# Loading the v weights of an attention and GLU kernel in quarters on two queues, and moving one small norm computation

## The chip, the cores and the metric

One core of a Trainium2 chip. The metric is device time in microseconds of one execution. Most executions agree to within a few tenths of a per cent, and this study is about a few tenths of a per cent, so the scatter itself becomes a subject below. All times inside a profile are microseconds from the start of the profiled span; the span is about 1.8 us shorter than the device time of the same execution.

## The reference, cut to what matters

```
x = A_x                                   # 2048 tokens x 512
xn = layernorm(x)
A: qkv = xn @ wqkv; softmax features of q and k per head (32 heads of 16); linear attention; @ wo
B: ((xn @ w_gate) * (xn @ w_up)) @ w_down # 512 -> 1792 -> 512
return x + A(xn) + B(xn)
```

Everything works on tiles of 128 tokens (16 tiles, numbered 0 to 15). Before a tile can be multiplied it is loaded, centred and transposed.

Of the kernel before, what the change touches and what calls it, by code (L numbers as in the profile page):

```python
# [13 lines left out]
PE, ACT, DVE, POOL, SP = "PE", "ACT", "DVE", "POOL", "SP"  # L14
# [6 lines left out]
NQ = D // 128  # L21
# [104 lines left out]
def _build(nc, es, A_x, A_wqkv, A_w_phi, A_wo, B_w_gate, B_w_up, B_w_down, out):  # L126
# [142 lines left out]
    def load_x(t0, n, eng=SP):  # L269
        o = sb("x", t0 * 512, n * 512).rearrange("p (t d) -> p t d", t=n)  # L270
        i = rows(x_flat, t0, n)
        sc.dma(eng, lambda e: e.dma_start(o, i), [], [("x", t) for t in range(t0, t0 + n)], n * 131072)
# [11 lines left out]
    wv_v = sb("wv", 0, NQ * 512).rearrange("p (q j) -> p q j", q=NQ)  # L284
    wo_v = sb("wo", 0, NQ * 512).rearrange("p (q j) -> p q j", q=NQ)
# [5 lines left out]
    def load_w(eng, o, i, key, nbytes):  # L291
        sc.dma(eng, lambda e: e.dma_start(o, i), [], [key], nbytes)
# [10 lines left out]
            load_w(eng, v[:, :, sl], src[:, sl].rearrange("(q p) f -> p q f", p=128), (("wg", "wu")[k], s),  # L303
                   1024 * n)

    def load_v(eng, h):
        i = A_wqkv[h * 256:(h + 1) * 256, 1024:1536].rearrange("(q p) j -> p q j", p=128)
        load_w(eng, wv_v[:, 2 * h:2 * h + 2, :], i, ("wv", h), 262144)


    def c_fn(e):
# [11 lines left out]
    sc.pin = True  # L323
    load_x(0, 1)
    load_x(1, 1, ACT)
    load_x(2, 2)
    load_v(SP, 1)
    load_gu(SP, 0, (1,))
    act(sbf("lnv", 0, 1), eps_f, ["eps"], ["pace"])
    load_v(ACT, 0)  # L330
    load_gu(ACT, 0, (0,))
    load_gu(SP, 1)
    load_w(SP, wphi_v, bass.AP(tensor=A_w_phi.tensor, offset=A_w_phi.offset, ap=[[16, 128], [2048, NQ], [1, 16]]),
# [32 lines left out]
    def misc_bank(w=2):  # L366
        misc[0] += 1
        return 2 + misc[0] % w
# [4 lines left out]
    def w_fold(w, dt, b=None):  # L373
        b = misc_bank() if b is None else b

        def fn(e):
            ins = None
            for jt in range(NQ):
                ins = e.matmul(bank(b, jt * 128, 128), lhsT=wT_v[:, w, jt, dt * 128:(dt + 1) * 128],  # L379
                               rhs=wbd_v[:, jt, :], start=True, stop=True)  # L380
            return ins
        sc.step(PE, fn, [("wT", w, jt) for jt in range(NQ)] + [("wbd", jt) for jt in range(NQ)], [("ps", b)], 4 * 60.0)
        act(Wp_v[:, w, dt, :], bank(b), [("ps", b)], [("Wp", w, dt)])
# [91 lines left out]
    def x_transpose(t, b, h=0, parts=1, eng=ACT):  # L475
        n = NQ // parts
        qs = slice(h * n, (h + 1) * n)

        def fn(e):
            ins = None  # L480
            for i in range(n):
                q = h * n + i
                ins = e.transpose(bank16(b, i * 128, 128), xn_tile(t)[:, q * 128:(q + 1) * 128], ident)  # L483
            return ins
        sc.step(PE, fn, [("xn", t, h), "ident"], [("ps", b)], n * 60.0)
        o = sb("xnT", 0, NQ * S_TOK).rearrange("p (q s) -> p q s", q=NQ)[:, qs, t * 128:(t + 1) * 128]
        i = bank16(b, 0, n * 128).rearrange("p (q s) -> p q s", q=n)
        w = [("xnT", t, h)] if parts == 2 else [("xnT", t)]
        if eng == ACT:
            act(o, i, [("ps", b)], w)  # L490
        else:
            dve(lambda e: e.tensor_copy(out=o, in_=i), [("ps", b)], w, n * 128)
# [45 lines left out]
    def v_matmul(t, b, hs=(0, 1)):  # L538
        for h in hs:
            mm(bank(b), [(xnT(q, t * 128, 128), wv_v[:, q, :]) for q in (2 * h, 2 * h + 1)],  # L540
               ([("xnT", t, h)] if t < 2 else [("xnT", t)]) + [("wv", h)], b, start=h == 0, stop=h == 1)

    def v_keep(t, b):
        raw = sbf("vraw", (t - 2) * 512, 512)
# [103 lines left out]
    def squares(src, i, after):  # L648
        j = squared[0] % 4
        squared[0] += 1  # L650
        junk = hT_v[:, NF - 8 + 2 * j:NF - 6 + 2 * j, 3 * 512:4 * 512]
        over = [("junk", j)] if squared[0] > 4 else []
        sc.prio = 2
        if src != "wg":
            v, col, key = {"wv": (wv_v, 14 + i, [("wv", i)]), "wo": (wo_v, 16 + i, ["wo"]),
                           "wd": (wd_v, 18 + i, ["wd"])}[src]
            act(junk, v[:, 2 * i:2 * i + 2, :], key + after + over, [("junk", j), ("ssq", col)], func=ACTF.Square,
                accum=ssq[:, col:col + 1])
        else:
            i_ap = wg_v[:, :, i * 256:(i + 1) * 256].rearrange("p (a b) c -> p a b c", a=2)  # L660
            key = [(src, k) for k, (lo, n) in enumerate(SLICES) if lo < (i + 1) * 256 and lo + n > i * 256]
            act(junk.rearrange("p a (b c) -> p a b c", b=2), i_ap, key + after + over, [("junk", j), ("ssq", i)],
                func=ACTF.Square, accum=ssq[:, i:i + 1])
        sc.prio = 1
# [61 lines left out]
    def d_scale():  # L726
        norms(14, (2, 2, 7), 24)
        caps()
# [70 lines left out]
    def combine_weights(k, what=("tw", "two")):  # L799
        over = {1: [("xn", i) for i in range(4)], 2: [("Wp", 1, q) for q in range(NQ)], 3: [],  # L800
                4: [("ek", i, j) for i in range(2) for j in range(2)]}[k]
        ov_o = [("wv", 0), ("wv", 1)] if k == 1 else []
        for name, t, blk, n, src, ov in (("tw", tw, wd_block, NK, [("wdh", i) for i in range(7)], over),
                                         ("two", two, wo_block, 2, [("woh", i) for i in range(2)], ov_o)):
            if name not in what:
                continue
            i0, i1 = {1: (blk(0, 1), blk(0, 0)), 2: (blk(1, 1), t[1]), 3: (blk(1, 1), blk(0, 1)),
                      4: (blk(1, 0), t[2])}[k]
            need = {1: [], 2: [(name, 1)], 3: [(name, 1)], 4: [(name, 2)]}[k]
            dve(lambda e, o=t[k], i0=i0, i1=i1: e.tensor_tensor(out=o, in0=i0, in1=i1, op=ALU.subtract), src + need,  # L810
                [(name, k)] + ov, n * 256, 0.52)
# [218 lines left out]
    ln_center(3)  # L1030
    v_matmul(0, 0, (0,))
    v_matmul(1, 1, (0,))
    x_transpose(2, 6)
    v_matmul(0, 0, (1,))
    v_matmul(1, 1, (1,))
    for t in range(ND):
        ln_moments(t)
    (g0a, u0a, g0b, u0b), gate0 = up_unit(*ups.pop(0), pairs, 2)
# [37 lines left out]
    def scales(t):  # L1076
        last = [("hT", *latest[0])] if latest[0] else []
        for src, i in {6: [("wv", 0), ("wv", 1)], 7: [("wd", 0), ("wd", 1), ("wd", 2)],
                       8: [("wd", 3), ("wd", 4), ("wd", 5)], 9: [("wd", 6), ("wo", 0), ("wo", 1)]}.get(t, ()):
            squares(src, i, last)  # L1080
        if 2 <= t < 6:
            for i in range(2 * (t - 2), min(7, 2 * (t - 1))):
                squares("wg", i, last)
        if t in (5, 6):
            moments(range(7 * (t - 5), 7 * (t - 4)), last)
        if t == 7:
            row_of_r2(last)
            wide_row()
        if 11 <= t < 14:
            scale_weights(todo[3 * (t - 11):3 * (t - 10)], last)  # L1090
        for k, what in {14: [(1, "tw")], 15: [(3, "tw")], 16: [(2, "tw")], 17: [(1, "two"), (3, "two"), (2, "two")]}.get(t, ()):
            combine_weights(k, (what,))
        if t == 12:
            halves.extend([to_half(1), to_half(2)])
        if t >= 12:
            half_step(1)
# [26 lines left out]
    for t in range(NT + 3):  # L1123
        if t == NT + 2:
            kv_acc(t - 3)
            kv_finish()
        if t < NT:
            features("ek", t, 1)
        if t % 2 == 0 and 4 + t < NT:
            ln_stats(4 + t, 2)  # L1130
        if t > 0:
            up()
        x_next(t + 4)
        if t == 11:
            d_scale()
        late_loads(t)
        if 2 <= t - 1 < ND:
            v_place(t - 1, None)
        elif ND <= t - 1 < NT:
            b = misc_bank()  # L1140
            v_matmul(t - 1, b)
            v_place(t - 1, b)
        if t in (9, 11) or 12 <= t < NT + 1:
            if t not in (14, 16):
                up()
            if t in (9, 11, 13):
                q_next()
        if t == 7:
            w_fold(0, 2)
        scales(t)  # L1150
        if t < 2:
            v_place(t, t)
        else:
            up()
            if t == 8:
                norms(0, (7, 1), 8)
                h_scale()
                scale_row()
            if 8 <= t < NT:
                q_next()  # L1160
            if 9 <= t < 14:
                normalise(range(3 * (t - 9), min(NF, 3 * (t - 8))), [("hT", *latest[0])])
            if 3 <= t < NT + 2:
                kv_acc(t - 3)
            if t < 9:
                up()
        if 4 < t < 8:
            w_fold(0, (0, 1, 3)[t - 5])
        if t == 8:
            scaled[0] = True  # L1170
# [228 lines left out]
```

## The kernel before: the parts that the change touches

The program records steps per engine and a list scheduler in the kernel orders them when the program is built. The order on PE (TensorE) is the recorded one; DVE (VectorE), ACT (ScalarE), POOL and SP are ordered by modelled costs. In the first phase everything is "pinned" to the recorded order. The loads are issued from the queues of SP and ACT:

```
    sc.pin = True
    load_x(0, 1)              # tile 0, SP, 128 KB
    load_x(1, 1, ACT)         # tile 1, ACT
    load_x(2, 2)              # tiles 2 and 3, SP, 256 KB
    load_v(SP, 1)             # second half of the v weights, 256 KB
    load_gu(SP, 0, (1,))      # up weights, first slice
    act(sbf("lnv", 0, 1), eps_f, ["eps"], ["pace"])
    load_v(ACT, 0)            # first half of the v weights, 256 KB
    load_gu(ACT, 0, (0,))     # gate weights, first slice, 256 KB
    ...
```

The first work of PE after the transposes of tiles 0 and 1. `v_matmul(t, b, hs)` is xn of tile t times the v weights in halves of the contraction, into PSUM bank b; `g0a` and `u0a` are gate and up matmuls of block 0 for tiles 0 and 1:

```
    v_matmul(0, 0, (0,))
    v_matmul(1, 1, (0,))
    x_transpose(2, 6)
    v_matmul(0, 0, (1,))
    v_matmul(1, 1, (1,))
    ...
    g0a()
    x_transpose(3, 7)
    v_matmul(2, 2)
    v_keep(2, 2)
    u0a()
    v_matmul(3, 3)
    ...
    g1a()
    u1a()
```

In the main loop, "slot" t is one pass. Feature matmuls, v matmuls and the small norm matmuls take PSUM banks 2 and 3 in turn; each call of `misc_bank()` hands out the other one:

```
    def misc_bank(w=2):
        misc[0] += 1
        return 2 + misc[0] % w
    ...
    for t in range(NT + 3):
        ...
            features("ek", t, 1)          # takes a bank; ACT reads it with two exponentials
        ...
        x_next(t + 4)                     # normalise tile t+4 (DVE) and transpose it (DMA)
        if t == 11:
            d_scale()                     # norm sums: a 128x11 matmul takes a bank; DVE reads it
        late_loads(t)                     # t == 5: the down weights, 1792 KB, and wo, 512 KB
        ...
            b = misc_bank()
            v_matmul(t - 1, b)
            v_place(t - 1, b)
```

## Time and profile before

| | kernel before |
|---|---|
| median | 215.07 us, 3 runs, 214.67 to 215.19 |
| profiled span | 213.1 us |
| PE busy | 208.8 us, 98% |
| granted PE clock | 1.0 |

The page of the kernel before, its head and two of its rows of 40 time slices (each digit is tenths of a slice that the engine was busy):

```profile
span 213.1 us, 4042 instructions
PE 208.8 (98%) x1476; PEld 125.5 (59%) x1476; DVE 169.6 (80%) x277; ACT 144.6 (68%) x350; POOL 109.5 (51%) x137
PE   8999999999999999999999999999999999999994
ACT  5698899975789999986879977664544444432220
```

PE is the bound. A busy PE can still have pauses that this row hides, because the ends of matmuls are modelled and overlap the next start. So I compared starts: a 128x512 matmul follows the last one after 216 ns where nothing makes it wait. Where a step is longer, the surplus is a pause. In this profile there are two pauses over 0.3 us after the transposes of tile 1: at the first v matmul, and in slot 11 at about 90 us.

The timeline of PE in the kernel before, in the head (columns: start, duration, engine, line, operation, operands, shape, count, and idle time before it with what ended that):

```profile
5.46 0.25 PE L1009 MATMUL ps<-const-bfloat16-1.0 128*128 128x128 bf16 x1
6.06 1.02 PE L247 MATMUL ps<-arena 128*128 128x512 bf16 x4 [0.35 <-ACT arena L228]
6.92 0.39 PE L483 MATMUL ps<-arena 128*128 128x128 bf16 x4
7.14 1.46 PE L247 MATMUL ps<-arena 128*128 128x512 bf16 x8
8.44 0.39 PE L483 MATMUL ps<-arena 128*128 128x128 bf16 x4
8.66 1.46 PE L247 MATMUL ps<-arena 128*128 128x512 bf16 x8
```

The line at 6.06 is the first v matmul; the one at 8.66 begins with v of tile 2. The releaser is given as ACT, but ACT's copy of tile 0 was done at 5.30 us by its semaphore, while the first v half landed at 5.92. It is a DMA wait. The issues of the first 3 us in the kernel before (last column: us from issue to landing):

```profile
arena<-in_A_x_dram SPq DMA_DIRECT2D x1, 256.0 KB, 4.1
arena<-in_A_wqkv_dram ACTq DMA_DIRECT2D x1, 256.0 KB, 4.7
arena<-in_A_wqkv_dram SPq DMA_DIRECT2D x1, 256.0 KB, 5.1
arena<-in_B_w_gate_dram ACTq DMA_DIRECT2D x1, 256.0 KB, 6.2
```

The timeline of PE in the kernel before, in slot 11 (the 128x11 line is the norm matmul; the next one is v of tile 10):

```profile
88.76 1.24 PE L247 MATMUL ps<-arena 128*128 128x512 bf16 x5
89.83 0.17 PE L247 MATMUL ps<-arena,const-bfloat16-1.0 128*128 128x11 bf16 x1
90.42 2.76 PE L247 MATMUL ps<-arena 128*128 128x512 bf16 x12 [0.42 <-ACT arena L228]
```

From 89.83 to 90.42 is a step of 0.59 us for a matmul that needs 0.03. The chain of waits of the kernel before, around the place (columns: start, us, what), shows what ACT itself hung on:

```profile
41.37 9.25 DMA arena<-arena
...
51.96 1.28 DVE arena L676 x2
53.24 1.12 DVE arena L515
...
74.66 11.39 ACT arena L228 x27
86.05 0.21 issue
86.26 4.12 ACT arena L228 x8
90.38 0.05 issue
90.42 6.22 PE ps L247 x28
```

Read upwards: PE was released by ACT at 90.38, ACT had worked without a pause on a backlog, the backlog came from DVE, and DVE from a DMA from SBUF to SBUF.

### The profile page before, as it was taken

Reading aid. Unit: us, or ns where it says so; the run is one execution under the profiler, and the core shown is the slowest. Engines: PE = TensorE matmul, PEld = TensorE weight load, DVE = VectorE, ACT = ScalarE, POOL = GpSimd, SP = SyncE. Lnnn points to the kernel's source line nnn. Section 1 sums busy time; section 2 is a strip of 40 time slices with the busy share of each in tenths; the row PEclk is TensorE's granted clock in tenths of the full one; section 3 lists DMA queues with packets and bytes.
Section 4 is the critical chain, followed back from the end, with each engine's and each line's share of the span. In section 5 each row is a group of like instructions: output and inputs, shape, how many; then the busy total and the mean of one; then the engine's idle time right before and its main releaser. Section 6 shows DMA issues by size and latency. Waiting matters only on the chain.

```text
span 213.1 us, 4042 instructions
## 1 busy us (share of the span) xinstructions
PE 208.8 (98%) x1476; PEld 125.5 (59%) x1476; DVE 169.6 (80%) x277; ACT 144.6 (68%) x350; POOL 109.5 (51%) x137
## 2 busy tenths in 40 slices
PE   8999999999999999999999999999999999999994
PEld 3574444444544444444444444556888898899883
DVE  4848999986995647588799999996888898898622
ACT  5698899975789999986879977664544444432220
POOL 4031454540320366996995892004549559558540
PEclk9999999999999999999999999999999999999999
DMA  5999960799100220331412250413375636537411
GB/s 178 292 303 373 236 103 0 130 348 140 25 3 0 38 60 3 52 63 37 77 25 49 49 102 0 115 56 53 44 83 123 168 79 154 136 89 175 123 49 49
DMA packets 49075, 22.29 MB, mean 105 GB/s; under 512 B 38048, under 2 KB 47392, under 8 KB 49056
## 3 DMA queue, kind: packets, MB, share of 16 engines
q1 hardware_dynamic: 48112, 21.39, 45.1%
q10 hardware_dynamic: 944, 0.66, 1.0%
q8 instruction: 11, 0.18, 0.4%
q14 instruction: 8, 0.07, 0.1%
HBM read 11.03 MB, written 2.10 MB: 62 GB/s over the span
## 4 chain that ended last, share of the span: by engine, by line
PE 70%; ACT 15%; DVE 7%; DMA 6%; issue 1%; DVEq 0%
PE ps L247 67%; ACT arena L228 15%; DMA arena<-arena 4%; DVE arena L676 2%; DVE arena L515 2%; PE ps L619 2%; DMA arena<-in_A_x_dram 1%; PE ps L561 1%; DVE arena L902 1%; PE ps L379 0%; PE ps L483 0%; DVE arena L463 0%; DVE arena L425 0%; DVE arena L403 0%; DVE arena L932 0%
## 5 line engine op out<-in xcount | busy, mean ns | idle before, releaser
L247 PE MATMUL ps<-arena 128*128 128x512 bf16 (+2 forms) x1160 | 199.9, 330 | 0.8 <-ACT arena L228 0.8
L247 PEld LDWEIGHTS ps<-arena 128*128 128x128 bf16 (+1 forms) x1160 | 110.8, 98 | 74.2 <-ACT arena L228 1.5
L228 ACT ACTIVATE arena<-ps 128x512 bf16<-128x512 f32 (+4 forms) x117 | 59.0, 543 | 10.8 <-PE ps L247 6.6
L228 ACT ACTIVATE arena<-arena 128x32 f32<-128x32 f32 (+9 forms) x131 | 53.4, 424 | 13.4 <-DVE arena L515 8.5
L902 DVE TENSOR_TENSOR arena<-ps,arena 128x512 f16<-128x512 f32 (+1 forms) x56 | 38.3, 683 | 12.5 <-ACT arena L228 7.3
L525 POOL TENSOR_TENSOR arena<-arena 128x1024 bf16<-128x1024 bf16 x16 | 31.7, 1989 | 27.0 <-ACT arena L228 26.9
L515 DVE TENSOR_REDUCE arena<-arena 128x64 f32<-128x1024 bf16 x32 | 38.2, 1212 | 7.2 <-ACT arena L228 7.0
L228 ACT ACTIVATE arena<-ps,arena 128x512 bf16<-128x512 f32 (+1 forms) x55 | 35.9, 672 | 10.2 <-PE ps L247 10.0
L863 POOL TENSOR_TENSOR arena<-arena 128x256 f16<-128x256 f16 x32 | 23.8, 755 | 14.6 <-DMA arena<-arena 13.4
L841 DVE TENSOR_TENSOR arena<-arena 128x896 f16<-128x896 f16 x32 | 26.0, 812 | 3.4 <-PE ps L247 3.4
L228 ACT ACTIVATE ps<-ps 128x256 f32<-128x256 f32 x24 | 8.8, 368 | 29.0 <-PE ps L247 27.0
L932 DVE SCALAR_TENSOR_TENSOR arena<-ps,arena 128x256 bf16<-128x256 f32 (+1 forms) x24 | 13.2, 566 | 8.8 <-PE ps L247 8.7
L781 POOL TENSOR_TENSOR arena<-arena 128x512 f16<-128x512 bf16 x14 | 16.3, 1174 | 7.0 <-DVE arena L902 4.8
L967 POOL TENSOR_TENSOR arena<-arena 128x512 f32<-128x512 f32 x8 | 9.5, 1191 | 16.9 <-ACT arena L228 16.9
L531 POOL TENSOR_TENSOR arena<-arena 128x512 bf16<-128x512 bf16 x16 | 17.0, 1060 | 0.8
L629 DVE TENSOR_TENSOR arena<-ps,arena 128x512 f16<-128x512 f32 x16 | 11.0, 686 | 1.3 <-ACT arena L228 0.5
L403 DVE BATCH_NORM_STATS2 arena<-arena 128x6 f32<-128x512 bf16 x16 | 10.4, 671 | 0.1
L529 POOL TENSOR_TENSOR arena<-arena 128x32 f32<-128x32 f32 x16 | 5.0, 315 | 9.6 <-ACT arena L228 5.6
L461 POOL TENSOR_SCALAR arena<-arena 128x1 f32<-128x1 f32 x12 | 3.0, 265 | 13.1 <-ACT arena L228 10.9
L676 DVE BATCH_NORM_STATS2 arena<-arena 128x6 f32<-128x512 bf16 x14 | 9.0, 682 | 0.0
L561 PEld LDWEIGHTS ps<-arena 128*128 128x128 bf16 x128 | 6.1, 97 | 3.5
L463 DVE TENSOR_SCALAR arena<-arena 128x512 bf16<-128x512 bf16 x12 | 5.4, 486 | 2.3 <-DMA arena<-arena 1.8
(55 smaller groups left out, 74.9 us busy)
## 6 DMA issues: line engine op xcount, KB each, us to landing
arena<-in_A_x_dram SPq DMA_DIRECT2D x9, 256.0 KB, 3.3
out_dram<-arena SPq DMA_DIRECT2D x15, 128.0 KB, 2.0
arena<-in_B_w_down_dram SPq DMA_DIRECT2D x1, 1792.0 KB, 9.6
arena<-in_A_x_dram SPq DMA_DIRECT2D x3, 512.0 KB, 4.8
arena<-arena SPq DMA_TRANSPOSE x44, 3.1
arena<-in_B_w_gate_dram SPq DMA_DIRECT2D x1, 640.0 KB, 8.6
arena<-in_B_w_up_dram SPq DMA_DIRECT2D x1, 640.0 KB, 9.8
arena<-in_B_w_gate_dram SPq DMA_DIRECT2D x1, 512.0 KB, 5.0
```

The costliest lines, as they stand in the source:

```text
L228: return sc.step(ACT, lambda e: e.activation(out=out_ap, in_=in_ap, func=func, scale=scale, **kw), reads, writes, 130.0 + 0.833 * n)
L247: ins = e.matmul(out_ap, lhsT=l, rhs=r, start=start and i == 0, stop=stop and i == npair - 1, **kw)
L515: dve(lambda e: e.tensor_reduce(out=sm, in_=e_v, axis=AX.X, op=ALU.add), [(name, s, 0), (name, s, 1)], [("sums", sr)], 1024)
L525: pool(lambda e: e.tensor_tensor(out=e_w, in0=e_w, in1=r_w, op=ALU.mult), [(name, s, 0), (name, s, 1), ("rs", n)], [(name, s, 0), (name, s ...
L531: pool(lambda e: e.tensor_tensor(out=e_v[:, :, 1, :], in0=e_v[:, :, 1, :], in1=rat[:, :, None].to_broadcast([128, H, 16]), op=ALU.mult), [ ...
L629: dve(lambda e: e.tensor_tensor(out=o_tile(t).rearrange("p (b h f) -> p b h f", b=2, f=16), in0=nd[:, :, :, 0:16], in1=w_v[:, r].unsqueeze ...
L676: dve(lambda e, i=i: e.bn_stats(wst[:, i, :], wu_chunks[:, i, :]), keys + after, [("wst", i)], 512)
L781: pool(lambda e, ft=ft: e.tensor_tensor(out=hH_v[:, ft, 0:512], in0=hT_v[:, ft, 0:512], in1=r2w, op=ALU.mult), [("hT", ft, 0), "r2w", ("x" ...
L841: dve(lambda e, k=k, i0=i0, i1=i1, op=op: e.tensor_tensor(out=s_block(p, k), in0=i0, in1=i1, op=op), ks + more, [s_key(p, k)] + over.get(k ...
L863: pool(lambda e, k=k, i0=i0, i1=i1, op=op: e.tensor_tensor(out=so_block(p, k), in0=i0, in1=i1, op=op), ks + [("so", p, m) for m in more], ...
L902: dve(lambda e: e.tensor_tensor(out=h_v[:, ft, sg * 512:(sg + 1) * 512], in0=bank(bu), in1=g, op=ALU.mult), [("ps", bu), ("g", s)] + ([("j ...
L932: dve(lambda e: e.scalar_tensor_tensor(out=o, in0=src, scalar=inv, in1=resid, op0=ALU.mult, op1=ALU.add), keys + [rkey, "inv"], [("ostg", ...
```

## The change

Its intent: the first v matmuls should not wait for tiles 2 and 3 to be loaded first; and the norm matmul of slot 11 should not take the PSUM bank that the v matmul needs next.

```
-    def load_v(eng, h):                      # halves of 256 KB, keys ("wv", h)
+    def load_v(eng, q):                      # quarters of 128 KB, keys ("wv", q)
...
     load_x(0, 1)
     load_x(1, 1, ACT)
-    load_x(2, 2)
-    load_v(SP, 1)
+    load_v(SP, 0)
+    load_v(ACT, 1)
+    load_x(2, 1)
+    load_v(ACT, 3)
+    load_v(SP, 2)
+    load_x(3, 1)
     load_gu(SP, 0, (1,))
     act(sbf("lnv", 0, 1), eps_f, ["eps"], ["pace"])
-    load_v(ACT, 0)
     load_gu(ACT, 0, (0,))
...
     v_matmul(0, 0, (0,))
     v_matmul(1, 1, (0,))
-    x_transpose(2, 6)
     v_matmul(0, 0, (1,))
     v_matmul(1, 1, (1,))
+    x_transpose(2, 6)
...
         x_next(t + 4)
-        if t == 11:
-            d_scale()
         late_loads(t)
...                                           # v matmul, up matmuls, q features
+        if t == 11:
+            d_scale()
         scales(t)
```

The places that read the v weights name the quarters instead of the halves; that is all of the rest.

More of the change, by code (lines that the diff above doesn't have):

```diff
@@ L304, in load_gu @@
                    1024 * n)
-    def load_v(eng, h):
-        i = A_wqkv[h * 256:(h + 1) * 256, 1024:1536].rearrange("(q p) j -> p q j", p=128)
-        load_w(eng, wv_v[:, 2 * h:2 * h + 2, :], i, ("wv", h), 262144)
+    def load_v(eng, q):
+        load_w(eng, wv_v[:, q, :], A_wqkv[q * 128:(q + 1) * 128, 1024:1536], ("wv", q), 131072)
     def c_fn(e):
@@ L540, in v_matmul @@
             mm(bank(b), [(xnT(q, t * 128, 128), wv_v[:, q, :]) for q in (2 * h, 2 * h + 1)],
-               ([("xnT", t, h)] if t < 2 else [("xnT", t)]) + [("wv", h)], b, start=h == 0, stop=h == 1)
+               ([("xnT", t, h)] if t < 2 else [("xnT", t)]) + [("wv", 2 * h), ("wv", 2 * h + 1)], b, start=h == 0, stop=h == 1)
     def v_keep(t, b):
@@ L654, in squares @@
         if src != "wg":
-            v, col, key = {"wv": (wv_v, 14 + i, [("wv", i)]), "wo": (wo_v, 16 + i, ["wo"]),
+            v, col, key = {"wv": (wv_v, 14 + i, [("wv", 2 * i), ("wv", 2 * i + 1)]), "wo": (wo_v, 16 + i, ["wo"]),
                            "wd": (wd_v, 18 + i, ["wd"])}[src]
@@ L801, in combine_weights @@
                 4: [("ek", i, j) for i in range(2) for j in range(2)]}[k]
-        ov_o = [("wv", 0), ("wv", 1)] if k == 1 else []
+        ov_o = [("wv", q) for q in range(NQ)] if k == 1 else []
         for name, t, blk, n, src, ov in (("tw", tw, wd_block, NK, [("wdh", i) for i in range(7)], over),
```

## The prediction

> **What bounds the kernel.** TensorE. The page gives PE 208.8 us busy of a 213.1 us span (98%), clock 1.0. Warm 128x512 matmuls follow each other every 216 ns. From the first v matmul at 6.06 us to the last matmul at 210.2 us (timeline) one hole over 50 ns breaks that rhythm: at 89.83 us, put down to ACT. Before 6.06 us is the head: the first tiles land at 3.37 and 3.53 us, transposes run from 4.48 to 5.6 us, then PE idles 0.35 us. The wait view calls the releaser ACT, but the ACT copy of tile 0 was done at 5.30 us; the v half that this matmul needs landed at 5.92 us (DMA list: 4.7 us from issue). So that is a DMA wait.
>
> **What the change does.** No arithmetic is added; two more DMA issues. Two effects:
>
> 1. Head. 512 KB must arrive before the first v matmul, not 768 KB. From the landings before (768 KB by 5.92 us, 1024 KB by 6.80) I estimate the first two v quarters at 4.5 to 5.0 us, the others at 6.0. Then v starts when transposes and copies let it, at 5.6 to 5.7 us, and its four groups (0.43 us each) run through to 7.4 us. Part is given back: tile 3 now lands at about 6.5 us instead of 5.35, and ACT's mean of it (0.63+0.2 us) stands ahead of the copy of tile 2's transposes; and the gate weights landed at 7.87 us before, needed at 8.0. I expect v of tile 2 at about 8.4 us (8.66 before). Net 0.2 us, between -0.1 and 0.45.
>
> 2. Slot 11. The norm matmul (128x11) took PSUM bank 2 of a rotation of two, so the next v matmul fell on bank 3 and waited for ACT's exponentials there, done at 90.38 us: a step of 0.59 us instead of nothing. With the norms later, it takes bank 2, whose exponentials were done at 89.40, before PE arrives (89.83). The hole of 0.56 us goes. The margin is 0.43 us, and ACT is 100% busy from 70 to 90 us, so a head gain beyond that may be lost again.
>
> **How much is critical.** The chain of waits runs over PE up to 35.5 us, then DVE, DMA transposes and ACT to 90.4, then PE to the end. Both effects lie on it, so they reach the end almost whole: 0.2 + 0.55 = 0.75 us of 215.07.
>
> Predicted 214.3 us, range 213.7 to 214.9. Faster by over 2%: 0.01; within 2%: 0.98; slower: 0.01.
>
> **What would show it.** Right: first v matmul at about 5.65 us without a DMA wait; v of tile 2 near 8.4; no PE step of 0.59 us near 90 us. Wrong: PE waits for gate weights or tile 3 near 7.5 to 8.5 us; a new hole between 89 and 97 us from ACT or DVE's norm reads.
>
> **What could make it wrong.** The Trainium skill ("TensorE: Matmul & The Clock Gate", Part 1) says that the array starts at half rate and is released by sustained activity. The trace agrees: 107 ns per 128-wide matmul until 5.46 us, 216 ns per 512-wide one from 6.06. If the release falls after 5.65 us, the earlier v matmuls win less. The extra issues delay everything behind them on the SP queue by some 0.5 us: tiles 4 to 7 landed at 14.88 us and DVE took them at 14.90, so later stages could slip.

## The result

| | before | changed |
|---|---|---|
| runs beside each other, median | 214.88 us, 4 runs | 214.41 us, 4 runs (214.32 to 214.98) |
| ratio | | 0.9983, 95% interval 0.996 to 1.0006 |
| second comparison, another chip | 214.73 us, 11 runs (214.26 to 216.11) | 214.71 us, 6 runs (214.43 to 215.18) |
| ratio | | 1.0001, 95% interval 0.9975 to 1.0027 |

A ratio is the mean time of one kernel's fast runs over that of the other's of the same rounds, so it is not quite the ratio of the medians quoted here. Neither interval excludes no gain at all.

The head of the page of the changed kernel:

```profile
span 212.6 us, 4025 instructions
PE 207.7 (98%) x1455; PEld 125.2 (59%) x1476; DVE 166.5 (78%) x277; ACT 144.6 (68%) x350; POOL 109.8 (52%) x137
```

The program has 1476 matmuls in both kernels; 21 records are missing in this trace. A missing record looks like a step that is one matmul too long, 432 ns for two of 216, and must not be read as a pause. PE's fall from 208.8 to 207.7 us means nothing for the same reason.

The timeline of PE in the changed kernel, in the head:

```profile
5.43 0.22 PE L1011 MATMUL ps<-const-bfloat16-1.0 128*128 128x128 bf16 x1
5.49 2.06 PE L247 MATMUL ps<-arena 128*128 128x512 bf16 x8
7.38 0.39 PE L485 MATMUL ps<-arena 128*128 128x128 bf16 x4
7.74 0.61 PE L247 MATMUL ps<-arena 128*128 128x256 bf16 x4
8.52 0.40 PE L485 MATMUL ps<-arena 128*128 128x128 bf16 x4 [0.17 <-DVE arena L451]
8.75 1.35 PE L247 MATMUL ps<-arena 128*128 128x512 bf16 x7
```

v starts 0.57 us earlier (5.49 against 6.06), yet v of tile 2 starts later (8.75 against 8.66). Three pauses have come in between, measured as steps over the dense rhythm: 0.17 us before the second half of v, whose third quarter landed at 6.44; 0.13 us before the gate matmuls, whose weights landed at 7.69; and 0.34 us before the transposes of tile 3 at 8.52. The last is a chain: tile 3 landed at 7.26 us, ACT averaged it, DVE centred it. The timelines of ACT and DVE in the changed kernel show it:

```profile
7.28 0.63 ACT L228 ACTIVATE arena<-arena 128x512 bf16<-128x512 bf16 x1 [1.26 <-DMA arena<-in_A_x_dram]
7.82 0.19 ACT L228 ACTIVATION_READ_ACCUMULATOR arena<-arena 128x1 f32 x1
8.11 0.35 DVE L451 TENSOR_SCALAR arena<-arena 128x512 bf16<-128x512 bf16 x1 [1.38 <-ACT arena L228]
```

In slot 11 of the changed kernel PE's timeline has one unbroken line, where the kernel before had the pause:

```profile
88.83 4.48 PE L247 MATMUL ps<-arena 128*128 128x512 bf16 x19
```

So the half microsecond by which the two profiled spans differ (213.1 and 212.6) comes from slot 11, and the head gave 0.09 us away. Taken at face value that is a finished explanation. The experiments show that it holds for these two executions and not for the kernels.

### The profile page after: what moved, and what is told of

Its sections match the earlier page's. It is cut to its first block, busy times and chain, and to the rows that moved or that the text cites. A ratio compares the mean times of both kernels' runs of the same rounds, so it can differ in the third digit from the quotient of the medians.

```text
span 212.6 us, 4025 instructions
## 1 busy us (share of the span) xinstructions
PE 207.7 (98%) x1455; PEld 125.2 (59%) x1476; DVE 166.5 (78%) x277; ACT 144.6 (68%) x350; POOL 109.8 (52%) x137
## 4 chain that ended last, share of the span: by engine, by line
PE 94%; DMA 2%; SPq 1%; issue 1%; DVE 0%; ACT 0%; DVEq 0%
PE ps L247 89%; DMA arena<-in_A_x_dram 2%; PE ps L563 2%; PE ps L621 2%; PE ps L381 1%; SPq L292 0%; SPq L272 0%; ACT arena L228 0%; DVE arena L934 0%; PE ps L485 0%; DVE arena L451 0%; DVEq L1359 0%
## 5 line engine op out<-in xcount | busy, mean ns | idle before, releaser
L247 PE MATMUL ps<-arena 128*128 128x512 bf16 (+2 forms) x1139 | 197.8, 329 | 1.1
L563 PEld LDWEIGHTS ps<-arena 128*128 128x128 bf16 x128 | 6.1, 97 | 3.5
L621 PEld LDWEIGHTS ps<-arena 128*128 128x128 bf16 x128 | 6.2, 97 | 1.2
```

The source lines that it names most:

```text
L247: ins = e.matmul(out_ap, lhsT=l, rhs=r, start=start and i == 0, stop=stop and i == npair - 1, **kw)
L621: ins = e.matmul(bank(b0 + c // 4, (c % 4) * CW, CW), lhsT=ph[:, c, :], rhs=kvz_v[:, c, :], start=True, stop=True)
```

## The experiments

Theory A: the slot 11 part is worth 0.55 us in every run, the head nothing. Theory B: the loads pay. Theory D came up after the first four runs: the pause in slot 11 is not a property of the program order alone, but appears only in an execution where a certain DMA lands late (measured against PE's own progress, as the table below shows).

Timing could not decide most of this: within one kernel the runs scatter by 0.4 to 1.9 us. The profiles could, because from the end of v of tile 2 on, PE's time to the last matmul is almost constant. In the plain variants it is 199.87 us in five profiles with the norm sums moved (after, a1, a2, e2, e3), 199.99 to 200.00 us in three without (b1, b2, e1), and 200.46 us in the first profile of before. So I read each profile at three places: the head, slot 11, and the last matmul.

### Head alone, slot alone (e1_head_only, e2_slot_only)

```
e1: the changed kernel, with        e2: the kernel before, with
-        if t == 11:                -        if t == 11:      # before late_loads
-            d_scale()              -            d_scale()
         scales(t)                  +        if t == 11:      # before scales
and d_scale() back after x_next     +            d_scale()
```

> Edit: the new loads and the new order of the first v matmuls, with the norm sums of slot 11 left where they were. Theory A (the whole gain comes from slot 11; the head's earlier start is lost again in three later waits of PE): no gain, -0.1 to +0.15 us against the kernel before; first v matmul near 5.5 us, v of tile 2 near 8.75 us, and the PE step of about 0.55 us at about 90 us still there. Theory B (the head's earlier loads are what pays): 0.3 to 0.6 us faster than before.

> Edit: the kernel before with only the norm sums of slot 11 moved. Theory A: 0.5 to 0.6 us faster than before, as fast as the whole change or 0.05 us faster; no PE step over 0.3 us near 90 us. Theory B: no gain, since ACT is busy throughout there and would only make PE wait a little later.

Measured: e1 ratio 0.9992 (0.9977 to 1.0007), e2 ratio 0.9994 (0.9975 to 1.0012). Both theories had asked for a visible gain from one of the two; neither has it. The profile of e1 has v starting at 5.71 and v of tile 2 at 8.70 us, so the head behaves as in the full change. But slot 11, in the old order, looks like this in PE's timeline of e1:

```profile
89.85 0.17 PE L247 MATMUL ps<-arena,const-bfloat16-1.0 128*128 128x11 bf16 x1
89.99 3.20 PE L247 MATMUL ps<-arena 128*128 128x512 bf16 x14
```

The step after the norm matmul is 0.14 us, not 0.59. Either the head repairs slot 11, or the 0.59 was an accident of one run. The profile of e2 has no pause in slot 11, but it ended later than before's (last matmul at 210.38 against 210.16), because the loads of its head landed later: the second v half at 7.66 us instead of 6.80, and the gate weights, which PE met last, at 8.76 instead of 7.87.

### How little must move (e3_norm_after_v)

```
-        if t == 11:                  # before late_loads
-            d_scale()
...
             v_matmul(t - 1, b)
             v_place(t - 1, b)
+        if t == 11:
+            d_scale()
```

> Edit: the kernel before, with the norm sums called directly after the v matmul of slot 11 instead of directly before it, so they move by one matmul group instead of eight. Theory A1 (the hole comes from the rotation of two PSUM banks: the norm matmul takes the free bank and pushes the v matmul onto the one that ACT still reads): the hole of 0.56 us goes, 0.5 to 0.6 us faster than before. Theory A2 (ACT and DVE are simply behind in this slot and PE must wait for them somewhere): a wait of 0.3 to 0.6 us stays within the next 5 us, gain under 0.2 us.

Measured: ratio 0.9991 (0.9975 to 1.0006). There is no pause near 90 us in the profile: letting the v matmul go first is enough, which supports A1: the bank rotation is where PE waits. Its time from v of tile 2 to the last matmul is 199.87 us, that of the full move. But in this execution ACT kept pace with PE (the exponentials were done at 90.05 us, 0.08 us before PE's group ended), so only a pause of about 0.12 us was there to remove. A2 is not tested here for an execution in which ACT is behind; e6 below is one. The size that A1 expected, 0.5 to 0.6 us, did not appear in the time. A more direct test, the norm sums in unused columns of PSUM bank 0 (DVE would read the bank while PE writes it, unordered), was not run.

### The same kernels again (b1_before_again, b2_before_again, a1_after_again, a2_after_again)

No edit: second and third profiles of the kernel before and of the changed kernel.

> The unchanged kernel before, a second profile. Theory D (the 0.56 us hole of slot 11 in the first profile is not a fixed cost but comes with a slow load of the down weights: 9.55 us to landing there, which held back a transposing DMA, then DVE, then ACT): where that load lands within about 9.1 us of its issue, the step after the 128x11 matmul is 0.1 to 0.2 us, not 0.59. Theory A: the step is 0.55 to 0.6 us again.

> The unchanged kernel before, a third profile, for the same question: step after the 128x11 matmul 0.1 to 0.2 us with a quick load of the down weights (theory D) or 0.55 to 0.6 us always (theory A). It also shows how far the landing of the second v half scatters: 6.80, 7.66 and 7.05 us in the three profiles so far that have the old loads.

> The changed kernel, timed again in five rounds with a second profile. If the gain is 0.55 us at slot 11 plus nothing at the head (theory A), 0.4 to 0.6 us faster than before. If slot 11 is worth only about 0.1 us in a usual run (theory D), 0.1 to 0.3 us faster. Head: v of tile 2 ends within 0.15 us of 9.75 us, with waits of PE before tile 3's transposes.

> The changed kernel, a third profile: third and fourth v quarters landed by 6.5 us (less scatter than the old second half), tile 3 between 7.2 and 7.4 us, no PE step over 0.3 us near 90 us whatever the down weights' load takes up to 9.6 us.

Measured: b1 214.34 us, b2 215.06 us, a1 a median of 214.71 us with the ratio 1.0001 given above, a2 214.94 us. PE's timeline of b1, the unchanged kernel before, in slot 11:

```profile
89.77 0.17 PE L247 MATMUL ps<-arena,const-bfloat16-1.0 128*128 128x11 bf16 x1
89.91 3.41 PE L247 MATMUL ps<-arena 128*128 128x512 bf16 x15
```

The step is 0.15 us in b1 and in b2: a surplus of 0.12 us, not 0.56. Theory A falls. There are five profiles with the old place of the norm sums if e8 below is left out, where a landing was pushed late successfully (before, b1, b2, e1 and e5); one of the five has the large pause. b1's span is 212.6 us, that of the changed kernel in its best-looking profile. Theory D's expected small step came in b1 and b2, but in b2 not for the expected reason. The load of b2 was quick from issue to landing (8.05 us) only because it was issued 1.45 us later than in before, and what waited behind it landed as late as in before (50.60 against 50.62 us); the pause stayed away because PE came 0.62 us later. a1 missed its head (v of tile 2 ended at 9.92 us, expected 9.75 within 0.15), and its medians show 0.02 us of gain, less than either theory asked for, with an interval too wide to decide between them. The expectation for a2 that the third and fourth quarters land by 6.5 us did not hold (7.06 us), nor did that of its tile 3 (7.88 us).

What decides? The v matmul waits for ACT's exponentials on bank 3. Their end against the landing of the transposing DMA of tile 10 (the expectations below call it the tenth tile's), which stands in the SP queue behind the load of the down weights, and against the end of PE's matmul group before the norm matmul, all read from semaphore times:

| profile | tile 10's transpose landed | exponentials done | difference | PE group ended |
|---|---|---|---|---|
| before | 50.62 | 90.38 | 39.76 | 90.01 |
| a1 (changed) | 50.59 | 90.36 | 39.77 | 90.21 |
| after (changed) | 50.28 | 90.01 | 39.73 | 90.09 |
| b1 | 50.03 | 89.87 | 39.84 | 89.94 |
| b2 | 50.60 | 90.56 | 39.96 | 90.63 |
| e1 | 49.78 | 89.94 | 40.16 | 90.03 |

The exponentials are done at the later of two times: 39.73 to 39.77 us after that landing (the chain of waits of before, which ran through DVE's and ACT's backlog), or 0.08 us before PE's own group ended (ACT keeping pace with PE). Of the profiles not in the table, a2, e2, e3 and e4 fit the second time (0.08 us before PE's group ended) and e7 the first (39.73 us after the landing); e5 and e6 below, in which the scheduler had changed the order of DVE and ACT, have 39.46 and 39.21 us and do not fit the first. In before PE was early and the landing late, so PE met ACT's backlog. In b1, b2 and e1 ACT kept pace, and only the 0.12 us remain. In a1 ACT was behind PE by 0.15 us again, but the changed kernel does not wait for those exponentials there, and has no pause. The chain of waits of b1 has no DMA, DVE or ACT between 39 and 97 us at all.

### Making the landing late (e5_ballast_before, e6_ballast_after, e8_ballast_same_order)

An extra DMA ahead of the load of the down weights, into a part of SBUF not yet used:

```
         elif t == 5:
+            ballast = hT_v[:, 0:2, 3 * 512:4 * 512]        # e8: 0:4, twice the bytes
+            src = B_w_down[0:256, :].rearrange("(f p) j -> p f j", p=128)
+            sc.dma(SP, lambda e: e.dma_start(ballast, src), [], [("hT", 0, 3), ("hT", 1, 3)], 262144)
             load_w(SP, wd_v, ..., "wd", 1835008)
```

A second part of the edit is cut here: it makes ACT's first pass over the down weights wait for the extra load too. In e8 the scheduler is told 0 bytes for the ballast and 1619008 for the down weights, which keeps its order on PE, ACT, DVE and POOL the same as in the kernel before; only its model of time changes, not the transfer.

> Edit: the kernel before with one more DMA of 256 KB (part of the down weights, into a place not yet used) issued just ahead of the down weights' load, so that this load and the transposing DMAs behind it land later. Theory D (a late load of the down weights opens the hole at slot 11): in the profiles so far ACT was done with the exponentials that the v matmul waits for at 41.7 us after the down weights landed, or at PE's own pace if that is later. With 1.0 to 1.3 us more, at about 49.2 to 49.9 us, the step after the 128x11 matmul grows to 1.0 to 1.7 us and the kernel is 0.8 to 1.5 us slower than before. Theory A (the hole is PE's and the rotation's alone): step unchanged, time unchanged within 0.3 us.

> Edit: the same extra DMA of 256 KB in the changed kernel. Theory D: there the v matmul of slot 11 waits for exponentials that are done 0.97 us earlier (about 40.8 us after the down weights landed), so of the same delay only 0 to 0.6 us reach PE: 0 to 0.6 us slower than the changed kernel, and 0.8 to 1.1 us faster than the kernel before with the same extra DMA. If moving the norm sums were worth only a constant 0.12 us, both kernels would slow down alike.

Measured: e5 ratio 0.9994 (0.9955 to 1.0034), e6 ratio 0.9986 (0.9955 to 1.0018). The 0.8 to 1.5 us expected of e5 did not come. Two reasons show in its profile: the down weights landed at 48.95 us, only 0.3 us later than in before, because that load itself had taken 9.55 us in before and took less here; and the scheduler had moved one DVE statistics step ahead of the step that waits, so DVE idled 0.4 us instead of 1.8. The step in slot 11 was 0.14 us. e5 therefore tests nothing. In e6 the landing did come late (52.14 us), the exponentials were done at 91.35 us, 0.62 us after PE's group, and the changed kernel had no pause there. The timeline of PE in e6, first in slot 11 and then at the norm matmul of slot 8 (128x8):

```profile
88.82 4.48 PE L247 MATMUL ps<-arena 128*128 128x512 bf16 x19
```

```profile
69.70 0.17 PE L247 MATMUL ps<-arena,const-bfloat16-1.0 128*128 128x8 bf16 x1
69.92 1.04 PE L247 MATMUL ps<-arena 128*128 128x512 bf16 x4
```

The second shows that this norm matmul, which the change does not move, now cost a step of 0.22 us, where it cost 0.03 in before and after. With another 0.04 us at 60 us, e6 took 200.15 us from v of tile 2 to the last matmul, not 199.87: the late landing was not free for the changed kernel. The expectation that e6 would be 0.8 to 1.1 us faster than e5 was missed (medians 214.68 and 214.94 us). The absence of a pause in slot 11 fits theory D, but without a matching run of the kernel before it is half a test.

> Edit: the kernel before with one more DMA of 512 KB ahead of the down weights' load, as in e5 but twice the size, and with the sizes that the program's own list scheduler is told changed so that the order of instructions on PE, ACT, DVE and POOL stays that of the kernel before (in e5 and e6 DVE's order had moved at just the place where it waits). Theory D: in the profiles where ACT was behind, it was done with the exponentials of slot 11 at 39.73 to 39.77 us after the tenth tile's transposing DMA had landed (50.62 us in the first profile of before), in all others later and 0.08 us before PE's preceding matmul group ended. The extra bytes put that landing at 52.0 to 53.2 us; the exponentials are then done at 91.8 to 93.0 us and the step after the 128x11 matmul is 1.5 to 2.9 us, less whatever PE already loses near 52 us while DVE waits; the kernel is 1.4 to 2.8 us slower than before. Theory A (a fixed cost of rotation and order): the step stays at 0.12 to 0.6 us and the time within 0.4 us.

Measured: 215.91 us (6 runs) against 215.13 (11 runs), ratio 1.0041 (1.0011 to 1.0071), the only ratio whose interval excludes 1. Waits of DVE between 40 and 62 us, first in before, then in b1, then in e8 (us in total, times, longest):

```profile
DVE arena L463 <- DMA arena<-arena: 1.8, 1, 1.8
```

```profile
DVE arena L463 <- DMA arena<-arena: 1.4, 2, 1.3
```

```profile
DVE arena L463 <- DMA arena<-arena: 3.3, 2, 2.9
```

The transpose of tile 10 landed at 51.74 us and the exponentials were done at 91.50 us: 39.76 us later, as in the first profile of before. PE's timeline of e8:

```profile
54.46 1.02 PE L247 MATMUL ps<-arena 128*128 128x512 bf16 x4
56.14 1.04 PE L247 MATMUL ps<-arena 128*128 128x512 bf16 x4 [0.66 <-DVE arena L904]
...
90.97 0.17 PE L247 MATMUL ps<-arena,const-bfloat16-1.0 128*128 128x11 bf16 x1
91.55 1.69 PE L247 MATMUL ps<-arena 128*128 128x512 bf16 x7 [0.41 <-ACT arena L228]
```

The pause of slot 11 is back, 0.58 us per step, although PE had already lost 1.07 us (0.82, 0.15 and 0.10) at 55 to 61 us to the same late DVE. The landing was 0.3 us short of what I had expected, and the time rose by 0.4% (0.9 us), less than the 1.4 to 2.8 us expected; most of what PE lost in the profile lies at 55 to 61 us, so the rise says little of slot 11. What stands is the trace: with the order of instructions the same on all four engines, an extra load that pushes the landing later opens the pause in slot 11, and at the offset read before. Beside it, e6 is close to the missing counterpart: ACT was 0.62 us behind PE's group in e6 and 0.36 us in e8 (91.50 against 91.14), and PE paused in slot 11 only with the old place of the norm sums. The two differ in the bytes added and in DVE's order, so it is not a strict control. What e8 does not give is how often an ordinary execution is in that state; one of three profiles of the unchanged kernel before was.

### Using the head's earlier start (e4_fill, e7_tile3_last)

```
e4, against the changed kernel:         e7, against the changed kernel:
-    x_transpose(2, 6)                  -    ln_mean(3); ln_center(3)   (before v)
+    x_transpose(2, 2)                  -    x_transpose(2, 6)
     ...                                +    x_transpose(2, 2); ln_mean(3); ...; ln_center(3)
     g0a()                                   ...
+    g1a()                                   g0a()
-    x_transpose(3, 7)                       v_matmul(2, 2); v_keep(2, 2)
+    x_transpose(3, 3)                  +    g1a(); x_transpose(3, 3)
     v_matmul(2, 2); v_keep(2, 2)            u0a()
     u0a()                              +    u1a()
     v_matmul(3, 3); v_keep(3, 3)            v_matmul(3, 3); v_keep(3, 3)
-    g1a()
     u1a()
```

> Edit: the changed kernel, with the first gate matmuls of block 1 (which need only tiles 0 and 1 and the gate weights of block 0) moved ahead of the transposes of tile 3, and the transposes of tiles 2 and 3 put on PSUM banks 2 and 3. Theory A (the head loses its earlier start because PE stands in front of tile 3, which lands at 7.26 us and is ready at 8.47): the wait of 0.34 us before tile 3's transposes goes; v of tile 2 at about 8.8 us with 0.43 us more work done by then; 0.3 to 0.4 us faster than the changed kernel, 0.8 to 0.9 us faster than before. If the gain of the head is instead taken back by ACT near 90 us, a new hole opens there and the time is that of the changed kernel.

> Edit: the changed kernel with tile 3 put last in the head: tile 2's transposes are copied before ACT averages tile 3, v of tile 2 and both first gate matmuls come before tile 3's transposes, v of tile 3 after both first up matmuls. Theory: the head loses its earlier start only because PE stands in order behind work that needs tile 3; then PE has no wait after the gate weights have landed, and ends 0.5 to 0.65 us earlier than the changed kernel at equal landings (last matmul at about 209.0 to 209.3 us in a run with quick loads): 0.4 to 0.7 us faster than before in the mean, under the 2% of a verdict. If the loads themselves bound the head, the waits only move to the third and fourth v quarter, the gate or the up weights, and the time is that of the changed kernel.

Measured: e4 214.41 us (214.01 to 215.17), ratio 0.9989 (0.997 to 1.0008); e7 214.26 us (214.16 to 215.83), ratio 0.9981 (0.9948 to 1.0013), each against before on its own chip. PE's timeline of e4:

```profile
7.52 1.04 PE L247 MATMUL ps<-arena 128*128 128x256 bf16 x8
8.65 0.40 PE L485 MATMUL ps<-arena 128*128 128x128 bf16 x4
8.89 2.54 PE L247 MATMUL ps<-arena 128*128 128x512 bf16 x14
```

Both gate groups (eight matmuls) are now done before tile 3's transposes, and the last matmul of the profile starts at 209.36 us, the earliest. In e1, in which the gate weights landed at about the same time (7.27 us there, 7.42 here), it is 209.73, of which 0.13 belong to slot 11. So e4 gains about 0.24 us in such an execution, less than the 0.3 to 0.4 expected, since a surplus of 0.26 us before tile 3 is left. e7's last matmul starts at 209.48 us and misses its expected 209.0 to 209.3: its v of tile 2 now comes so early that it waits 0.40 us for ACT's copy of tile 2:

```profile
8.34 1.48 PE L247 MATMUL ps<-arena 128*128 128x512 bf16 x8 [0.24 <-ACT arena L228]
```

Neither is shown to be faster than either kernel; their medians are lower than those of before beside them by 0.25 and 0.83 us, inside the scatter.

### What bounds the head

Putting all profiles of the two ways to load together (without e4 and e7, which reorder PE's work in the head), the head sorts itself by one landing, that of the first gate weights:

| loads | profile | first v starts | gate weights landed | v of tile 2 ends | difference |
|---|---|---|---|---|---|
| old | b1 | 5.77 | 7.40 | 9.65 | 2.25 |
| old | before | 6.06 | 7.87 | 9.71 | 1.84 |
| old | e8 | 5.85 | 7.97 | 9.73 | 1.76 |
| old | e3 | 5.87 | 8.08 | 9.84 | 1.76 |
| old | e5 | 5.96 | 8.43 | 10.19 | 1.76 |
| old | b2 | 5.91 | 8.58 | 10.34 | 1.76 |
| old | e2 | 6.07 | 8.76 | 10.52 | 1.76 |
| new | e1 | 5.71 | 7.27 | 9.74 | 2.47 |
| new | after | 5.49 | 7.69 | 9.80 | 2.11 |
| new | a1 | 5.63 | 7.88 | 9.92 | 2.04 |
| new | e6 | 5.55 | 8.42 | 10.18 | 1.76 |
| new | a2 | 5.62 | 8.65 | 10.42 | 1.77 |

Where the gate weights land at 7.97 us or later, v of tile 2 ends 1.76 to 1.77 us after them with either way to load: the first gate matmuls stand in PE's order ahead of it, and whatever PE gained before them it spends waiting. The change does not reduce the bytes that land ahead of the gate weights (tiles 0 to 3 and all of v in both kernels; in the changed one tile 3 is issued after them, at 2.65 us against 2.24, and still landed first). The new loads start v 0.33 us earlier in the mean (5.60 against 5.93), and v of tile 2 ends at 10.01 us in the mean of five against 10.00 in the mean of seven. No gain of the head shows, though ends that range from 9.65 to 10.52 us leave room for a tenth or two either way. Where the gate weights land early, the new loads even lose: with landings of 7.87 and 7.88 us, v of tile 2 ends at 9.71 in before and at 9.92 in a1, where PE waits 0.26 us before the transposes of tile 3, which landed at 7.38 us (tiles 2 and 3 landed at 5.35 in before). The landing of the same gate weights moves by 1.5 us between executions (7.27 to 8.76), and it accounts for most of the difference between profiled executions: b1 with 7.40 took 214.34 us, b2 with 8.58 took 215.06. What moves it is not known. Loading the gate weights first, ahead of v, is the rival order, and it was not tried.

## Why the prediction was right or wrong

The number was right: 214.3 predicted with a range of 213.7 to 214.9, 214.41 measured, and "within 2%". It came out partly by luck, because one of its two terms was the size of a pause in the one execution of the kernel before that had been profiled, and the other did not materialise. The gain foretold was 0.75 us; the medians of the two comparisons differ by 0.47 and 0.02 us. The stated range was also wide enough to hold the kernel before itself (214.88 us beside it), so landing in it says little. And the prediction's own sign of being wrong came: PE waited for the gate weights (0.13 us) and for tile 3 (0.34 us) between 7.5 and 8.5 us. Part by part:

- **PE bounds, and what PE gains reaches the end.** Right. From the end of v of tile 2 to the last matmul took 199.87 us in five profiles, to within 0.01.
- **Head, first v at 5.6 to 5.7 us.** Right, 5.49 to 5.71 us in five profiles with these loads. The estimate of 4.5 to 5.0 us for the first two quarters was near (4.39 and 4.65), that of 6.0 for the others less so (5.60 and 6.44).
- **Head, net 0.2 us.** Mis-sized: it measured 0.0 us (10.01 against 10.00 in the means above). The step that failed is "tile 3 now lands at about 6.5 us instead of 5.35", which was 7.26 in the profile, and, more, "the gate weights landed at 7.87 us before, needed at 8.0". I took this landing as fixed and just early enough. It moves by 1.5 us and in seven of the twelve profiles it alone set the pace. v of tile 2 started at 8.75 us, not 8.4.
- **Slot 11, 0.55 us.** The mechanism, the rotation of two PSUM banks, was right as far as the runs go: e3 shows no pause with the v matmul first, and e6 none with the norm sums moved although ACT was 0.62 us behind. The size was wrong: the term measured 0.13 us (200.00 less 199.87) in the ordinary case, and 0.59 us (200.46 less 199.87) only in the one execution that the first profile happened to show. The failing step is "a step of 0.59 us instead of nothing", read as a property of the program. The chain of waits above it named a DMA at 41 to 50 us as the origin; DMA times vary between executions, so the size of such a pause does too. e8 shows the same pause opened by an extra load that makes the landing later, with the order of instructions unchanged.
- **Margin of 0.43 us, new waits from ACT or DVE's norm reads.** None appeared; the norm matmul in its new place had a step of about 0.03 us.
- **Clock.** Named as a risk, and it is one, though a small one: in e1 and e6 the array was still at half rate when v began, which cost 0.16 and 0.27 us there.
- **Later stages slipping for the extra issues.** Did not show: tiles 4 to 7 landed at 14.82 us against 14.88 in the first profiles, and at 14.72 to 15.52 against 14.59 to 15.37 in the twelve of the table.

My estimate of the true gain, from these profiles, is therefore the sum of the terms: 0.0 + 0.13 us where the gate weights land late, about nothing where they land early (there the head loses about what slot 11 gains), and more, up to the 0.59 us seen in slot 11, where the landing behind the down weights is late against PE. That is below what these runs can resolve by timing; the two ratios, 0.9983 and 1.0001, allow it. How often the late state occurs stays open.

## What to carry to other kernels

A pause in one profile has the size of that execution; before counting it as a saving, follow the chain of waits to its start, and if it starts at a DMA, profile the same kernel two or three times more. Before moving a load forward, find the last thing that the stage waits for: here it was the gate weights and not the v weights in seven of twelve profiles, and the two orders of the loads before them landed them at 8.16 and 7.98 us in the mean, a difference well inside their scatter. And where engines take buffers in turn, a small instruction placed out of turn costs little while the reader keeps pace, but makes the next large one wait as soon as the reader falls behind.

## What the Trainium skill lacked or had wrong

- "TensorE: Matmul & The Clock Gate", Part 1, says that the array leaves half rate around 4 us into sustained matmuls, give or take 0.5 us from run to run, with a free-running window. The spread here was wider than that; the same part also reports that one kernel's count of slow matmuls changed from 6 to 11 to 14 between runs, which is nearer to it. Whether the window makes the spread is not shown here. By the step between matmuls, the release fell at about 3.4 to 3.7 us in e3, a1 and e2, at 5.0 to 5.5 us in e7, b1, after and a2, and at 6.0 to 6.1 us in e1 and e6 (in the others a pause of PE hides it), always with the first matmul at 0.82 us: 2.6 to 5.3 us after it. (PE paused for some 0.3 us or more at about 4.2 us, waiting for the first tile, so the activity was not quite unbroken.)
- "DMA: Bandwidth & Descriptors", section "Issuing engines are not separate DMA queues", says that DMAs issued from different engines run on the same 16 engines and interleave, so that issuing from several saves only issue time. The runs are in line with it and are no test of it: in the changed kernel a tile on SP and a v quarter on ACT, issued at 1.71 and 1.72 us, landed at 5.42 and 5.60 us, and the gate weights behind them gained nothing beyond the scatter. The page gives a fixed cost and a rate for a DMA (fitted for DMAs issued from GpSimd, while these come from SP and ACT) but no scatter between executions: the same 256 KB of gate weights landed between 7.27 and 8.76 us, and the same 1792 KB of down weights took 7.9 to 9.6 us from issue to landing.
- No page that I read says how a trace with missing matmul records looks: 21 of 1476 were missing in the profile of the changed kernel, each leaving a step that is one matmul too long (such as 432 ns in place of two of 216).
